# Score matmuls of a gated attention kernel: two on row halves at once, the third of a group over all 128 rows, the VectorE path's over all 128 rows, heads in alternating order

## The chip, the cores and the metric

The kernel runs on one core of one Trainium2 chip. The metric is device time in microseconds (us). Runs of one kernel on a chip are quoted as a median, and each is labelled fast when it lies within 1.5% of the fastest run of its kernel; only fast runs enter the ratios. A profile is of one execution; its span is about 2 us shorter than the measured time (1023.4 of 1025.38 us before).

## The reference

For x of 2048 x 512, the output is g * A(x) + (1 - g) * B(x) with g = sigmoid(x . gate_w).

- A is softmax attention with 32 heads of 16 channels: `scores = q k^T / 4`, `p = softmax(scores)`, `o = p v`, then a 512 x 512 output projection. The 32 x 2048 x 2048 exponentials are the bulk of all work.
- B is linear attention over softmax features of q and k, 32 features per head, with its own projections.

Everything is bf16 at the interface.

## The kernel before

Attention works on tiles of four heads and 512 queries (n counts the tiles, 32 in all). For each block of 128 keys, one score matmul per head writes a 128 x 512 result, which I call a unit. ScalarE exponentiates most units; of each tile's sixteen key blocks, one or two go to VectorE, which computes an approximate exponential. I call that the VectorE path: 224 of the 2048 units.

The ring of score results is a PSUM tile of 128 x 5 x 512 f32. I call each of its five parts of 128 x 512 a bank, so a unit fills one. Units go through it in groups of three and two banks in turn, and ScalarE takes one group per instruction:

```python
RING = 5
GROUPS = (3, 2)
...
deps = [self.o_exp[k - 2] if k >= 2 else None]      # a group's matmuls wait for the exp two groups back
...
def qk(x):
    n, kt, i = units[x]
    g = n % NG
    j = 64 * (i // 2)                               # heads 0, 1: rows 0-63; heads 2, 3: rows 64-127
    return lambda e: e.matmul(
        self.ps_ring[:, x % RING, :], self.kT[j:j + 64, g // 2, kt * P:(kt + 1) * P],
        self.qT[j:j + 64, n % 4, i % 2, :], start=True, stop=True, tile_position=(j, 0))
...
self.o_exp.append(s.op("act", ..., lambda e: e.activation(       # one exp over 3 or 2 banks
    self.ET[:, s0:s0 + w, :], self.ps_ring[:, b0:b0 + w, :], ACT.Exp, scale=float(DH) ** -0.5),
    deps, prio=tu))
```

kT holds the keys of eight heads, sixteen rows each. q of one head is stored with zeros in the other rows, so that a matmul over 64 rows of kT gives one head's scores. In the trace of before, two such matmuls on different row halves start 3 to 7 ns apart, so I take them to run at the same time; two on the same half start 219 to 227 ns apart. With heads in the order 0, 1, 2, 3, the halves run 0, 0, 1, 1, so half of the two-bank groups meet one half twice.

The value matmuls (17 columns: 16 channels and the row sum) take four heads side by side in four column quarters of the array; in the trace of before most of these start 3 or 4 ns after one another. A scheduler in Python puts all instructions into a fixed order per engine before the program is built; it uses assumed durations.

The softmax here doesn't subtract the row's maximum and nothing guards it: scores larger than these inputs give would overflow.

## Time and profile before

| | before |
|---|---|
| time | 1027.74 us, median of 3 (1026.12 to 1034.1) |
| span of the profile | 1023.4 us |
| mean granted TensorE clock | 0.832 |
| ScalarE at its own pace | 846 us |
| start and tail | 24 us |
| lost by ScalarE at full clock | 66 us of 683 |
| lost by ScalarE at half clock | 87 us of 317 |

The last four rows are worked out from the starts of ScalarE's instructions in the trace. I took the time from each start to the next. The first tenth of these times is ScalarE's own pace: 1.33 us after a three-bank exp, 0.90 us after a two-bank one, 0.48 us after a feature exp. Whatever is longer is lost, and it is booked under the clock that was granted at the later of the two starts, when the wait ends.

The page of the profile, cut to the header and the slices (one digit per fortieth of the span; PEclk is the granted clock in tenths):

```profile
span 1023.4 us, 12592 instructions
...
PE 882.4 (86%) x5216; PEld 220.3 (22%) x5216; DVE 774.7 (76%) x1082; ACT 881.6 (86%) x797; POOL 6.6 (1%) x12
...
ACT  4678578889888998899988989989899889999895
...
PEclk9878878898777888789988979957589698878775
```

Read ACT and PEclk together: ScalarE's thin slices stand where the clock is low. The costliest groups, with shapes kept apart (busy us, mean ns of one, then the idle time before them and what ended it):

```profile
L565 ACT ACTIVATE ET<-ps_ring 128x1536 bf16<-128x1536 f32 x365 | 539.6, 1478 | 100.3 <-PE ps_ring L551 95.1 <-PE ps_ot L585 2.5 <-PE ps_mp L615 0.8
L551 PE MATMUL ps_ring<-qT,kT 64*128 64x512 bf16 x1824 | 484.1, 445 | 100.7 <-ACT ET L565 95.3 <-DVE kT L492 2.3
L565 ACT ACTIVATE ET<-ps_ring 128x1024 bf16<-128x1024 f32 x364 | 383.5, 1053 | 17.6 <-PE ps_ring L551 12.5 <-PE ps_ot L585 3.9
```

Most of ScalarE's idle time stands before three-bank exps (100.3 us, against 17.6 before two-bank ones). (The means overlap a little: a three-bank exp lasts 1478 ns in the mean, and at ScalarE's own pace the next exp starts 1.33 us after its start.) Now five stretches from the table of stretches (PE, weight load, VectorE, ScalarE, GpSimd busy, then the granted clock):

```profile
130.00:300.00 170.00, 151.97 (x866) 37.24 (x865) 136.54 (x176) 145.43 (x136) 0.00 (x0) 0.83 0.01 3
300.00:500.00 200.00, 172.91 (x1033) 43.32 (x1031) 162.82 (x218) 180.74 (x168) 0.00 (x0) 0.86 0.01 4
500.00:700.00 200.00, 177.01 (x1099) 45.84 (x1096) 166.46 (x245) 182.91 (x167) 0.00 (x0) 0.87 0.02 7
700.00:900.00 200.00, 174.82 (x1059) 43.88 (x1055) 165.17 (x239) 182.61 (x166) 0.00 (x0) 0.83 0.02 6
...
950.00:975.00 25.00, 24.00 (x125) 4.97 (x121) 8.37 (x14) 21.77 (x20) 0.00 (x0) 0.73 0.00 1
```

The last row is the odd one: TensorE counts as busy for 24.0 of 25 us, and yet its clock is at half for part of the time. (The ends of matmuls are modelled in the profile, and a matmul at half clock counts as busy for longer: the median of a 64-row one is 606 ns, against 386 at full clock.) Long idle gaps aren't what stands there: from 130 us to 25 us before the end, no gap between TensorE's matmuls is longer than 1.3 us, and yet 82 windows of half clock lie in that stretch. The record of the granted clock knows in this trace only 1.0 and 0.5, in multiples of 3.413 us (but for the last entry, where the record ends); I call a stretch of 3.413 us on this grid a window.

What half clock does to a three-bank group, from the timeline (start, length, instructions, and in brackets the idle time before and what ended it; first at full clock, then at half; the last line is three exps in a row, with the form of the first):

```profile
501.96 0.60 PE L551 MATMUL ps_ring<-qT,kT 64*128 64x512 bf16 x3 [0.63 <-ACT ET L565]
```
```profile
956.64 1.04 PE L551 MATMUL ps_ring<-qT,kT 64*128 64x512 bf16 x3 [0.47 <-ACT ET L565]
...
957.71 4.03 ACT L565 ACTIVATE ET<-ps_ring 128x1536 bf16<-128x1536 f32 x3 [0.21 <-PE ps_ring L551]
```

Three matmuls take 0.60 us at full clock and 1.04 at half, and then ScalarE waits for them. The loop is: three-bank exp, its banks free, the next three-bank scores, the next three-bank exp. At full clock its fastest passage is 1.50 + 0.64 = 2.14 us. One pair of exps takes ScalarE 1.33 + 0.90 = 2.235 us, so TensorE has about 0.1 us to spare. I call this its slack.

### The profile page before, as it was taken

What the parts mean: (1) busy time and instruction counts of PE and PEld (TensorE: products, weight loads), DVE (VectorE), ACT (ScalarE), POOL (GpSimd) and SP (SyncE); (2) the same over time, 40 slices, a digit from 0 to 9 for tenths busy, and PEclk for the clock granted to TensorE, in tenths of its full rate; (3) what the DMA queues carried; (4) which work ended last, traced back from release to release, by engine and by line L of the source; (5) the groups of instructions that cost most, each with busy time, mean ns of one, the idle gap of its engine ahead of it and who ended that gap; (6) DMA issues with size and microseconds to landing.
All of it is one profiled execution on the core that took longest, in us unless ns stands there. A gap on an engine that the chain in (4) does not pass through costs nothing.

```text
span 1023.4 us, 12592 instructions
## 1 busy us (share of the span) xinstructions
PE 882.4 (86%) x5216; PEld 220.3 (22%) x5216; DVE 774.7 (76%) x1082; ACT 881.6 (86%) x797; POOL 6.6 (1%) x12
## 2 busy tenths in 40 slices
PE   6699888898889888988888898899988898888986
PEld 2122221222121221222222222212222222211111
DVE  3676787789777897789878979878788789877271
ACT  4678578889888998899988989989899889999895
POOL 2000000000000000000000000000000000000000
PEclk9878878898777888789988979957589698878775
DMA  5500000000000000000000000000000000000000
GB/s 124 126 6 2 1 6 1 6 1 1 6 1 6 1 1 5 1 6 6 11 6 11 6 6 11 11 1 1 2 5 1 5 16 12 3 3 1 1 1 21
DMA packets 25240, 11.25 MB, mean 11 GB/s; under 512 B 18080, under 2 KB 25184, under 8 KB 25184
## 3 DMA queue, kind: packets, MB, share of 16 engines
q1 hardware_dynamic: 23600, 10.06, 3.8%
q8 instruction: 41, 0.67, 0.3%
q10 hardware_dynamic: 1584, 0.39, 0.2%
q14 instruction: 15, 0.12, 0.0%
HBM read 3.16 MB, written 2.10 MB: 5 GB/s over the span
## 4 chain that ended last, share of the span: by engine, by line
PE 46%; ACT 43%; DVE 6%; SPq 4%; issue 1%; DMA 1%; ACTq 0%
ACT ET L565 40%; PE ps_ring L551 21%; PE ps_ot L585 8%; PE ps_mp L455 7%; PE ps_mp L615 3%; ACT phi L766 3%; PE ps_mp L845 3%; SPq L396 2%; PE ps_ot L644 1%; SPq L416 1%; DVE EW L621 1%; DVE ED L636 1%; DVE Ef L626 1%; DVE Em L631 1%; DVE Et L632 1%
## 5 line engine op out<-in xcount | busy, mean ns | idle before, releaser
L565 ACT ACTIVATE ET<-ps_ring 128x1536 bf16<-128x1536 f32 x730 | 850.8, 1265 | 117.9 <-PE ps_ring L551 107.6
L551 PE MATMUL ps_ring<-qT,kT 64*128 64x512 bf16 x1824 | 484.1, 445 | 100.7 <-ACT ET L565 95.3
L621 DVE TENSOR_SCALAR EW<-ps_mp 128x512 int32<-128x512 f32 x224 | 148.4, 682 | 86.6 <-PE ps_mp L615 75.9
L585 PE MATMUL ps_ot<-ET,Vaug 128*17 128x512 bf16 x1824 | 205.3, 443 | 4.8 <-DVE Vaug L502 2.2
L551 PEld LDWEIGHTS ps_ring<-qT,kT 64*128 64x128 bf16 x1824 | 86.0, 97 | 334.7 <-ACT ET L565 253.2
L636 DVE SCALAR_TENSOR_TENSOR ED<-EW,Et 128x1024 uint16<-128x1024 int32 x112 | 134.2, 1202 | 0.5 <-PE ps_ot L644 0.4
L615 PE MATMUL ps_mp<-qT,kT 64*128 64x512 bf16 x224 | 91.8, 440 | 13.1 <-DMA qT<-qst 7.4
L585 PEld LDWEIGHTS ps_ot<-ET,Vaug 128*17 128x17 bf16 x1824 | 44.1, 88 | 221.9 <-issue 201.4
L626 DVE TENSOR_SCALAR Ef<-EW 128x2048 f16<-128x2048 uint16 x56 | 68.2, 1218 | 1.2
L631 DVE TENSOR_TENSOR Em<-Ef,Em 128x2048 f16<-128x2048 f16 x56 | 68.1, 1216 | 0.0
L632 DVE TENSOR_TENSOR Et<-Et,Em 128x2048 f16<-128x2048 f16 x56 | 67.9, 1213 | 0.2
L655 DVE STREAM_TRANSPOSE T_79<-ps_ot 128x512 f32<-128x512 f32 x32 | 22.8, 713 | 57.8 <-PE ps_ot L585 57.4
L455 PE MATMUL ps_mp<-xT,WA 128*128 128x512 bf16 x128 | 43.5, 441 | 8.2 <-DMA xT<-in_A_x_dram 7.4
L766 ACT ACTIVATE phi<-ps_mp 128x512 bf16<-128x512 f32 x64 | 34.8, 599 | 9.9 <-PE ps_mp L455 9.9
L455 PE MATMUL ps_mp<-Wp,xT 128*128 128x512 bf16 x128 | 42.3, 415 | 0.9 <-DVE ob L810 0.9
L770 DVE TENSOR_REDUCE fsum<-phi 128x64 f32<-128x1024 bf16 x32 | 38.8, 1212 | 3.9 <-ACT phi L766 3.8
L772 DVE TENSOR_TENSOR phi<-phi,frec 128x1024 bf16<-128x1024 bf16 x32 | 38.8, 1212 | 0.0
L628 DVE TENSOR_SCALAR Em<-Ef 128x2048 f16<-128x2048 f16 x56 | 38.1, 680 | 0.7
L629 DVE TENSOR_SCALAR Et<-Ef 128x2048 f16<-128x2048 f16 x56 | 38.2, 682 | 0.0
L615 PEld LDWEIGHTS ps_mp<-qT,kT 64*128 64x128 bf16 x224 | 20.1, 97 | 67.1 <-issue 30.9
L644 PE MATMUL ps_ot<-ED,Vaug 128*17 128x512 bf16 x224 | 27.4, 502 | 1.4 <-DVE ED L636 1.4
L455 PE MATMUL ps_mp<-WA,xT 128*128 128x128 bf16 (+1 forms) x128 | 22.8, 298 | 3.2 <-DVE qT L471 1.7
(63 smaller groups left out, 375.9 us busy)
## 6 DMA issues: line engine op xcount, KB each, us to landing
out_dram<-outt SPq DMA_DIRECT2D x16, 128.0 KB, 1.7
qT<-qst SPq DMA_DIRECT2D x124, 16.0 KB, 1.8
WA<-in_A_wqkv_dram SPq DMA_DIRECT2D x3, 384.0 KB, 4.8
WBV<-in_B_wqkv_dram SPq DMA_DIRECT2D x1, 512.0 KB, 4.6
WoA<-in_A_wo_dram SPq DMA_DIRECT2D x1, 512.0 KB, 5.3
WoB<-in_B_wo_dram SPq DMA_DIRECT2D x1, 512.0 KB, 6.1
WA<-in_A_wqkv_dram ACTq DMA_DIRECT2D x3, 128.0 KB, 3.4
xT<-in_A_x_dram SPq DMA_TRANSPOSE x16, 2.7
```

The costliest lines, as they stand in the source:

```text
L455: m = s.op("pe", self.c_mm(n), lambda e, c=c: e.matmul(self.bk(b)[:, 0:n], lhs(c), rhs(c), start=(c == 0), stop=(c == 3)), deps if c == 0 ...
L551: return lambda e: e.matmul(self.ps_ring[:, x % RING, :], self.kT[j:j + 64, g // 2, kt * P:(kt + 1) * P], self.qT[j:j + 64, n % 4, i % 2, ...
L565: self.o_exp.append(s.op("act", w * 0.427 + 0.09, lambda e, b0=b0, s0=s0, w=w: e.activation(self.ET[:, s0:s0 + w, :], self.ps_ring[:, b0:b ...
L585: return lambda e: e.matmul(self.ps_ot[32 * i:32 * i + VSL, :], self.Vaug[:, kt, h, :], self.ET[:, (4 * p + i) % NSLOT, :], start=(kt == 0 ...
L615: m = s.op("pe", self.c_mm(512), lambda e, i=i, b=b: e.matmul(self.bk(b), self.kT[64 * (i // 2):64 * (i // 2) + 64, cp, kt * P:(kt + 1) * ...
L621: ws.append(s.op("dve", 0.76, lambda e, i=i, b=b: e.tensor_scalar(self.EW[:, ew.idx, i * QCH:(i + 1) * QCH], self.bk(b), float(EC), float( ...
L626: f = s.op("dve", 1.13, lambda e: e.tensor_scalar(self.Ef[:], lo(), float(2.0 ** -16), None, op0=ALU.mult), ws + [self.ed_prev], pr)
L631: u = s.op("dve", 1.13, lambda e: e.tensor_tensor(self.Em[:], self.Ef[:], self.Em[:], ALU.mult), [m1], pr)
L632: g_ = s.op("dve", 1.13, lambda e: e.tensor_tensor(self.Et[:], self.Et[:], self.Em[:], ALU.mult), [t, u], pr)
L636: vs.append(s.op("dve", 1.13, lambda e, c0=c0: e.scalar_tensor_tensor(out=self.ED[:, ed.idx, c0], in0=self.EW[:, ew.idx, c0], scalar=float ...
L766: ex.append(s.op("act", 0.53, lambda e, sg=sg: e.activation(self.phi[:, ph.idx, :, sg, :], self.bk(b).rearrange("p (h f) -> p h f", f=DH), ...
L770: rd = s.op("dve", 1.15, lambda e: e.tensor_reduce(self.fsum[:, fs.idx, :], flat(), AX.X, ALU.add), ex, r + 10)
```

## The change

The intent is to have TensorE do the score matmuls in pairs, and to have the third matmul of a group address all 128 rows. For that q is stored in a layout padded with zeros over all eight heads, with two buffers instead of four. The heads of a tile are taken in the order 0, 2, 1, 3, so that neighbours lie on different halves. The score matmuls of the VectorE path also go over all 128 rows. The core of the diff:

```diff
+ORDER = (0, 2, 1, 3)
...
-        at("qT", [P, 4, 2, QCH], bf)
+        at("qT", [P, 2, 4, QCH], bf)
...
-        units = [(n, kt, i) for n in range(NN) for kt in range(NT) if kt not in dve_tiles(n) for i in range(4)]
+        units = [(n, kt, i) for n in range(NN) for kt in range(NT) if kt not in dve_tiles(n) for i in ORDER]
...
-            def qk(x):
+            def qk(x, half):
                 n, kt, i = units[x]
                 g = n % NG
-                j = 64 * (i // 2)
+                r = slice(64 * (i // 2), 64 * (i // 2) + 64) if half else slice(0, P)
                 return lambda e: e.matmul(
-                    self.ps_ring[:, x % RING, :], self.kT[j:j + 64, g // 2, kt * P:(kt + 1) * P],
-                    self.qT[j:j + 64, n % 4, i % 2, :], start=True, stop=True, tile_position=(j, 0))
-            o_qk = s.op("pe", 0.36, [qk(x) for x in range(ua, ub + 1)], deps, prio=-1e5 + k, cols=256 * (ub - ua + 1))
+                    self.ps_ring[:, x % RING, :], self.kT[r, g // 2, kt * P:(kt + 1) * P],
+                    self.qT[r, n % 2, i, :], start=True, stop=True, tile_position=(r.start, 0))
+            w = ub - ua + 1
+            o_qk = s.op("pe", 0.25 if w == 2 else 0.47, [qk(x, w > 1 and x < ua + 2) for x in range(ua, ub + 1)],
+                        deps, prio=-1e5 + k, cols=512 if w == 2 else 1024)
...                                                        # the VectorE path
-                self.bk(b), self.kT[64 * (i // 2):64 * (i // 2) + 64, cp, kt * P:(kt + 1) * P],
-                self.qT[64 * (i // 2):64 * (i // 2) + 64, n % 4, i % 2, :], start=True, stop=True,
-                tile_position=(64 * (i // 2), 0)),
+                self.bk(b), self.kT[:, cp, kt * P:(kt + 1) * P], self.qT[:, n % 2, i, :], start=True, stop=True),
```

Cut: the placement of q in the new layout (by transfer, and for the first tile by four VectorE multiplies from SBUF, 0.35 us each, in place of two from PSUM at 0.74 us), and the matching order of the value matmuls. The new assumed durations (0.25 and 0.47 instead of 0.36) also reorder the instructions on every engine; `cols` is not read by the scheduler.

## The prediction

> **What bounds the kernel now.** ScalarE, whenever TensorE delivers in time. The groups of instructions show 729 exps, at best 1.33 us (three banks) or 0.90 us (two) from start to start; with 64 feature exps that is 846 us of work in a span of 1023. Start and tail take 24 us. The other 153 us are waits, mostly for the next score matmuls (table of waits: ScalarE behind ps_ring), and they follow TensorE's clock. The granted clock is 1.0 or 0.5, in multiples of 3.413 us; 0.5 holds for 34% of the span (mean 0.832). Half-clock stretches lose 87 us of 317, full-clock ones 66 of 683; some 30 us of that are start-up stalls (at 47 and 101 to 130 us), which stay. Long full-clock stretches (458 to 516 us) lose only some 2%.

> **What sets the clock.** I counted each window's matmul columns, weighted by the share of the array they address (64 rows 1/2; 17-column value matmuls 1/4). Of 196 full-clock windows one value, about 2,960[...], separates those followed by half clock from the others, with one exception. [...]this trace asks for array area.

> **What the change does.**
> - Activity: per five units the score matmuls count 4 x 256 + 512 = 1,536 instead of 1,280, and VectorE's 224 score matmuls 512 each instead of 256: 1.245 million columns instead of 1.094. Spread evenly over ScalarE's minimum time in program order, 13% of windows lie below 2,960 before, 4% after. Half-clock windows averaged 2,835, just too little to get out; 12% more lets most leave after one or two.
> - Two-bank groups always run on both halves (starts 3 ns apart); before, half of them serialised (219 ns). ScalarE hardly waits for these at full clock.
> - Cost: between 64-row and 128-row matmuls 306 to 316 ns pass from start to start instead of 216[...]. In three-bank groups the last starts 308 ns after the first instead of 226: +85 ns on the loop exp, scores, exp, which takes 2.14 us of a cycle of 2.235. Its slack is just eaten, so every TensorE delay ahead of such a group becomes a ScalarE wait; at half clock it costs some 150 ns. VectorE's score matmuls no longer run beside a ring pair: up to 45 us more TensorE time, mostly idle time.
> - Start: four small SBUF multiplies for two PSUM evictions, under 0.5 us.

> **Prediction.** Half clock falls to about 10%, mean clock 0.95. 846 work + 24 ends + 55 to 60 lost at full clock (20 to 30 of it start-up) + 28 lost at half clock = about 957 us; range 930 to 992. Faster by over 2%: 0.94; within 2%: 0.05; slower: 0.01.

> **What would show it.** Mean clock over 0.92; few half-clock windows after 130 us; ScalarE's wait for ps_ring down from 108 to 40-60 us; first to last start 308 ns in three-bank groups, 3 ns in two-bank ones; ScalarE's mean exp unchanged.

> **What would make it wrong.** If the throttle does not count the 128-row matmul's added rows, the clock stays at 0.83 and the time at 1020 to 1045. If the lost slack bites at every three-bank group, 975 to 995. If VectorE (775 us busy) cannot keep the faster pace, its value matmuls stall.

846 + 24 + 55 to 60 + 28 is 953 to 958, for which I put 957.

## The result

The changed kernel takes 973.02 us (median of 4, 972.26 to 974.33). Beside it, before had a median of 1030.49 us. The ratio is 0.9445, 95% interval 0.94 to 0.9491. Ratios here are the mean time of one kernel's fast runs over that of the other's of the same rounds, so not quite the ratio of the medians. The changed kernel is 5.6% faster, and the time lies in the predicted range, 16 us above its point of 957.

The same lines of the profile after, first the page:

```profile
span 972.5 us, 12590 instructions
...
PE 805.8 (83%) x5216; PEld 241.9 (25%) x5216; DVE 771.3 (79%) x1081; ACT 874.1 (90%) x797; POOL 6.6 (1%) x10
...
ACT  4688579899999999999999998999999999898895
...
PEclk9898799999999899999999998999999999878795
```

The costliest groups by shape:

```profile
L574 ACT ACTIVATE ET<-ps_ring 128x1536 bf16<-128x1536 f32 x365 | 531.4, 1456 | 64.8 <-PE ps_ring L558 60.8 <-PE ps_ot L595 0.8
L574 ACT ACTIVATE ET<-ps_ring 128x1024 bf16<-128x1024 f32 x364 | 373.6, 1026 | 16.0 <-PE ps_ring L558 12.3 <-PE ps_ot L595 3.5
L558 PE MATMUL ps_ring<-qT,kT 64*128 64x512 bf16 x1458 | 298.0, 405 | 118.6 <-ACT ET L574 112.8 <-DVE kT L494 2.1 <-DVE qT L470 0.4
...
L558 PE MATMUL ps_ring<-qT,kT 128*128 128x512 bf16 x366 | 149.8, 409 | 0.0
```

The stretches:

```profile
130.00:300.00 170.00, 146.66 (x942) 43.50 (x942) 150.42 (x193) 158.85 (x151) 0.00 (x0) 0.98 0.01 3
300.00:500.00 200.00, 167.23 (x1127) 50.51 (x1126) 174.91 (x238) 192.49 (x179) 0.00 (x0) 0.97 0.02 5
500.00:700.00 200.00, 168.85 (x1130) 51.40 (x1130) 168.96 (x253) 190.12 (x174) 0.00 (x0) 0.96 0.02 6
700.00:900.00 200.00, 168.01 (x1073) 49.03 (x1073) 162.98 (x231) 187.81 (x171) 0.00 (x0) 0.93 0.02 6
```

And a three-bank group, at full and at half clock (the view prints the form of the first matmul; the third has 128 rows):

```profile
503.80 0.71 PE L558 MATMUL ps_ring<-qT,kT 64*128 64x512 bf16 x3 [0.17 <-ACT ET L574]
```
```profile
874.66 1.15 PE L558 MATMUL ps_ring<-qT,kT 64*128 64x512 bf16 x3 [0.47 <-ACT ET L574]
```

The reader should see three things. The clock is up from 0.83-0.87 to 0.93-0.98 in every stretch, although TensorE's busy time fell from 882 to 806 us, 86 to 83% of the span; the mean clock over the span is 0.938. ScalarE's busy time per stretch rose with the clock (180.7 to 182.9 us of each 200 before, 187.8 to 192.5 after). And each three-bank group became slower, not faster: 0.71 us instead of 0.60 at full clock, 1.15 instead of 1.04 at half. The added time stands between the second matmul (64 rows) and the third (128 rows), 318 to 320 ns from start to start at full clock where two 64-row matmuls on the same half have 219 to 227; I call that step a mode switch.

| term of the span, us | before | predicted | after |
|---|---|---|---|
| ScalarE at its own pace | 846 | 846 | 853 |
| start and tail | 24 | 24 | 24 |
| lost at full clock | 66 | 55 to 60 | 55 |
| lost at half clock | 87 | 28 | 40.5 |
| sum | 1023 | 957 | 972.5 |

How the losses divide between the two clocks depends on the booking. Cut at 130 us, start-up loses 37 us before and 34 after. From there on half clock loses 69 us before and 19 after, full clock 48 and 44. Booked under the clock at the earlier start instead, the same stretch loses 88 and 21 at half clock, 29 and 41 at full. So the fall at half clock, 50 to 67 us, stands either way; whether full clock lost less or more doesn't.

### The profile page after: what moved, and what is told of

Read it like the earlier page. It is cut to its first block, busy times and chain, and to the rows that moved or that the text cites. A ratio compares the mean times of both kernels' runs of the same rounds, so it can differ in the third digit from the quotient of the medians.

```text
span 972.5 us, 12590 instructions
## 1 busy us (share of the span) xinstructions
PE 805.8 (83%) x5216; PEld 241.9 (25%) x5216; DVE 771.3 (79%) x1081; ACT 874.1 (90%) x797; POOL 6.6 (1%) x10
## 4 chain that ended last, share of the span: by engine, by line
ACT 47%; PE 35%; DVE 10%; SPq 5%; DMA 2%; issue 1%; ACTq 0%
ACT ET L574 44%; PE ps_ring L558 16%; PE ps_ot L595 6%; PE ps_mp L453 6%; PE ps_mp L625 3%; PE ps_mp L853 3%; ACT phi L774 3%; SPq L398 2%; DVE EW L629 2%; DMA qT<-qst 2%; SPq L483 1%; SPq L418 1%; DVE ED L644 1%; DVE Et L640 1%; DVE Em L639 1%
## 5 line engine op out<-in xcount | busy, mean ns | idle before, releaser
L558 PE MATMUL ps_ring<-qT,kT 64*128 64x512 bf16 (+1 forms) x1824 | 422.3, 406 | 118.6 <-ACT ET L574 112.8
L558 PEld LDWEIGHTS ps_ring<-qT,kT 64*128 64x128 bf16 (+1 forms) x1824 | 105.7, 94 | 423.9 <-ACT ET L574 259.5
L595 PE MATMUL ps_ot<-ET,Vaug 128*17 128x512 bf16 x1824 | 187.8, 404 | 2.5 <-ACT ET L574 1.3
L625 PE MATMUL ps_mp<-qT,kT 128*128 128x512 bf16 x224 | 85.2, 402 | 22.5 <-DMA qT<-qst 13.7
L453 PE MATMUL ps_mp<-xT,WA 128*128 128x512 bf16 x128 | 40.5, 415 | 8.5 <-DMA xT<-in_A_x_dram 7.4
L453 PE MATMUL ps_mp<-Wp,xT 128*128 128x512 bf16 x128 | 37.6, 382 | 0.6 <-DVE ob L818 0.3
L625 PEld LDWEIGHTS ps_mp<-qT,kT 128*128 128x128 bf16 x224 | 20.2, 97 | 65.7 <-issue 27.0
L652 PE MATMUL ps_ot<-ED,Vaug 128*17 128x512 bf16 x224 | 23.9, 420 | 2.7 <-DVE ED L644 2.5
```

What stands on the lines that cost most here:

```text
L453: m = s.op("pe", self.c_mm(n), lambda e, c=c: e.matmul(self.bk(b)[:, 0:n], lhs(c), rhs(c), start=(c == 0), stop=(c == 3)), deps if c == 0 ...
L558: return lambda e: e.matmul(self.ps_ring[:, x % RING, :], self.kT[r, g // 2, kt * P:(kt + 1) * P], self.qT[r, n % 2, i, :], start=True, st ...
L595: return lambda e: e.matmul(self.ps_ot[32 * i:32 * i + VSL, :], self.Vaug[:, kt, h, :], self.ET[:, (4 * p + k) % NSLOT, :], start=(kt == 0 ...
L625: m = s.op("pe", self.c_mm(512), lambda e, i=i, b=b: e.matmul(self.bk(b), self.kT[:, cp, kt * P:(kt + 1) * P], self.qT[:, n % 2, i, :], st ...
```

## The experiments

### Old matmuls in the new order

```diff
-ORDER = (0, 2, 1, 3)
+ORDER = (0, 1, 2, 3)
-... [qk(x, w > 1 and x < ua + 2) for x in range(ua, ub + 1)]
+... [qk(x, True) for x in range(ua, ub + 1)]
 # VectorE path: back to 64 rows
```

> The changed kernel's placement of q and its instruction order, but every score matmul on 64 rows again and the heads in their old order, so the addressed array area is that of before (1.094 million weighted columns). If the gain comes from the array area (my theory): mean granted clock 0.80 to 0.86, 1010 to 1045 us. If it comes from the new instruction order or the new q placement: about 973 us, clock near 0.94.

1030.82 us, ratio 1.0104 (1.0028 to 1.018), clock 0.816 in the profile. The new order and layout bring nothing; if anything they cost 1%. That rival falls.

### Pairs only

```diff
-... [qk(x, w > 1 and x < ua + 2) for x in range(ua, ub + 1)]
+... [qk(x, True) for x in range(ua, ub + 1)]
 # VectorE path: back to 64 rows; ORDER stays (0, 2, 1, 3)
```

> Heads alternate halves, all score matmuls on 64 rows: two-bank groups run as pairs, area as before. Area theory: clock 0.80 to 0.87, 1000 to 1035 us. Rival (the two matmuls at once and the shorter TensorE time are the gain): 960 to 985 us with the clock still low; three-bank groups last 226 ns from first to last start.

1012.6 us (997.16 to 1026.16), ratio 0.9821 (0.9694 to 0.9948), clock 0.861 in the profiled run and 0.811 to 0.838 in the others:

```profile
PEclk9798999899677887989789999899979996657775
```

Two of its four runs are slow and don't enter the ratio. Pairing alone gave 2.8% against the old matmuls by the two ratios, 18 us by the medians of all runs; the spread is wide, and most of the gain is missing. By the traces, its own gain lies at half clock: 69 us lost there against 113, while at full clock both lose 55 to 57. But the profile caught the fastest run of this kernel and the slowest of the other, so these two figures overstate it.

### Third matmul wide, VectorE path narrow

```diff
 # VectorE path: back to 64 rows; all else as the changed kernel
```

> As the changed kernel, but the VectorE path's score matmuls on 64 rows: 93 of the 151 thousand added columns stay. Area theory: clock between a2 and the changed kernel, 0.89 to 0.93, 978 to 1000 us. If only the ring's matmuls matter: 973 us as the changed kernel. If the shared rows of the VectorE path cost TensorE time that hurts: faster than 973 us.

980.85 us, ratio 0.9592 (0.9518 to 0.9667), clock 0.92. The third matmul's added rows are worth 2.3% over the pairs alone by the ratios (32 us by the medians), and the rows added in the VectorE path about 8 us more, by the changed kernel's 973; that second step compares chips and isn't shown by itself. Both steps go with the clock: 0.811 to 0.861, 0.917 to 0.931, 0.938 to 0.944 over each kernel's runs. The first of them is the cleanest test of the rows, for the number of matmuls and their columns stay the same.

### Swap: wide matmuls in the two-bank groups

```diff
-... [qk(x, w > 1 and x < ua + 2) for x in range(ua, ub + 1)]
+... [qk(x, w == 3) for x in range(ua, ub + 1)]
```

> The 128-row matmuls moved to the two-bank groups (both of them), three-bank groups all on 64 rows: area 1,792 per five units instead of 1,536, no mode switch inside a three-bank group (226 instead of 322 ns from first to last start), two-bank groups serial (216 ns instead of 3). Area theory with the eaten slack: clock 0.95 to 0.98, waits of ScalarE in full-clock stretches lower by 5 to 15 us, 945 to 962 us. Rival (pairing the two-bank groups is the gain): slower than 973 us, 985 or more.

960.66 us (956.99 to 962.49), ratio 0.9401 (0.9346 to 0.9456), clock 0.968. One part of my expectation missed: the time lost at full clock is 57.5 us, not less than the changed kernel's 55. What fell are the half-clock losses (33 instead of 40.5 us) and ScalarE's own pace (846 instead of 853 us). Run again beside the changed kernel on one chip:

> The swap kernel again beside the changed kernel on one chip: 955 to 964 us, clock about 0.97, so 1.0 to 1.6% faster than the changed kernel; if the earlier difference came from the chip, within 0.5% of it.

959.3 us, ratio 0.9365 (0.9324 to 0.9407).

> The changed kernel again, for a comparison on one chip: 968 to 978 us, clock about 0.94.

972.65 us, ratio 0.9494 (0.9444 to 0.9544). The six runs of each don't overlap (957.78 to 959.88 and 970.14 to 974.93); the medians are 1.4% apart. So the swap is the better form, and pairing the two-bank groups isn't needed for it. Its groups in the timeline: two-bank matmuls 128 rows wide, three-bank groups back at 0.60 us.

```profile
500.23 0.60 PE L558 MATMUL ps_ring<-qT,kT 128*128 128x512 bf16 x2
...
501.58 0.60 PE L558 MATMUL ps_ring<-qT,kT 64*128 64x512 bf16 x3
...
502.61 0.59 PE L558 MATMUL ps_ring<-qT,kT 128*128 128x512 bf16 x2
```

### Useless work: two-bank groups issued twice

```diff
-... [qk(x, w > 1 and x < ua + 2) for x in range(ua, ub + 1)]
+... [qk(x, True) for _ in range(2 if w == 2 else 1) for x in range(ua, ub + 1)]
```

> All score matmuls of the ring on 64 rows, and both matmuls of every two-bank group issued twice, the second time for nothing (the same result written again): the area of a4_swap, 1,792 per five units, by useless work. Area theory: clock 0.95 to 0.98 and within 1% of the swap kernel of this call, though 728 more matmuls than in a2_pairs_only (1013 us) run. Rival (less TensorE work or matmuls on all 128 rows are what helps): no faster than a2_pairs_only, clock 0.87 or less.

966.15 us, ratio 0.9438 (0.9391 to 0.9485), clock 0.979. It runs 728 more matmuls than the pairs-only kernel, whose results are thrown away, and is 46 us faster by the medians (ratios to before 0.9438 and 0.9821, on two chips):

```profile
span 966.0 us, 14046 instructions
...
PEclk9899799999999999999999999999999999999997
...
L558 PE MATMUL ps_ring<-qT,kT 64*128 64x512 bf16 x2552 | 444.4, 386 | 93.0 <-ACT ET L574 87.2 <-DVE kT L494 2.1 <-DVE qT L470 0.7
```

No ring matmul has 128 rows here, so it isn't that form that helps. More array area per window went with a higher clock (0.974 to 0.982 over the runs here, 0.811 to 0.861 with pairs only); TensorE's saved time is not the gain. Issuing twice also fills TensorE's time, so this run alone doesn't tell area from busy time; the count of windows below does. The kernel is 0.7% slower than the swap although its clock is a little higher: from 130 us on it loses 54 us at full clock where the swap loses 44. So extra TensorE work isn't free either.

### Everything wide: the mode switch back in the loop

```diff
-... [qk(x, w > 1 and x < ua + 2) for x in range(ua, ub + 1)]
+... [qk(x, w == 3 and x < ua + 2) for x in range(ua, ub + 1)]
```

> Both matmuls of a two-bank group and the third of a three-bank group on 128 rows: area 2,048 per five units, but the mode switch is back in the loop of the three-bank groups (322 instead of 226 ns). The clock should be no lower than in the swap kernel (0.965 or more). If the eaten slack of that loop costs time at full clock: 5 to 15 us slower than the swap kernel of this call. If it does not: equal within 3 us or faster.

965.22 us, ratio 0.9421 (0.9377 to 0.9465), clock 0.98: 5.9 us slower than the swap at no lower a clock. ScalarE's own pace is 853 us here as in the changed kernel, against 846 in the swap. At full clock at least 90% of the three-bank exps start 36 or 37 ns after the end of their last matmul, so they wait for it nearly every time; in the swap the median is 58 ns. This is the price of the eaten slack: about 7 us in the pace. From 130 us on the waits at full clock are 6 us longer too (50.5 against 44), and 5 us come back at half clock (3.5 against 8), so the 5.9 us are what is left of a larger price.

### Swap with the VectorE path narrow

```diff
 # as the swap; VectorE path: back to 64 rows
```

> The swap kernel with the VectorE path's score matmuls back on 64 rows: 57 thousand weighted columns less (1.281 instead of 1.338 million, still more than the changed kernel's 1.245), and these matmuls can run beside ring matmuls again. Area theory: clock 0.95 to 0.97, 957 to 966 us, so no gain over the swap kernel's 959 to 961. If the 128-row form of these matmuls costs TensorE time on the chain of waits: 950 us or less.

961.37 us, ratio 0.9371 (0.9337 to 0.9404), clock 0.96. No gain over the swap, whose ratios were 0.9401 and 0.9365 on the other two chips. The 45 us of TensorE time that I thought the wide form could cost doesn't show on the chain of waits.

### Swap with the old head order

```diff
-ORDER = (0, 2, 1, 3)
+ORDER = (0, 1, 2, 3)
 # wide matmuls as in the swap
```

> The swap kernel with the heads in the old order: the area of the swap kernel, but no group owes anything to alternating halves (two-bank groups are serial on 128 rows, three-bank groups need two turns in any order). If area alone is the gain: 955 to 966 us, clock 0.96 to 0.98. If alternating the halves is a cause of its own at full clock: 970 us or more.

959.79 us, ratio 0.9361 (0.9327 to 0.9395), clock 0.974. The same time as the swap's 959.3 to 960.66, across chips: the alternating order, half of the change's idea, isn't needed once the wide matmuls stand in the two-bank groups.

### The changed kernel without alternating heads

```diff
-ORDER = (0, 2, 1, 3)
+ORDER = (0, 1, 2, 3)
```

> The changed kernel with the heads in the old order: same area, but half of the three-bank groups now have both 64-row matmuls on the same half, so that their last matmul starts about 540 ns after the first instead of 322. Loop of these groups 2.47 us against ScalarE's 2.25: about 0.2 us on 182 groups, 1000 to 1012 us, with the clock still at 0.92 or more. If the clock falls to 0.87 or less instead, pairs and not area hold it up.

1044.21 us (1033.14 to 1052.61, two of six runs slow), ratio 1.0131 (1.0078 to 1.0184), clock 0.918 in the profile. The clock, 0.892 to 0.927 over the six runs, came out a little under the 0.92 that I expected and well over 0.87; the time missed by more than 30 us. In its profile (1033 us) ScalarE lost 106 us at full clock instead of 55, in some 185 waits over 60 ns before three-bank exps (86 in the changed kernel), where I had expected 182 late groups. I had put the added loss at about 40 us and it is 51 at full clock, with 8 more at half. A late group from the timeline, 0.92 us long:

```profile
706.82 0.92 PE L558 MATMUL ps_ring<-qT,kT 64*128 64x512 bf16 x3 [0.69 <-ACT ET L574]
```

So a high clock alone doesn't make the kernel fast: at 0.918 this kernel is no faster than before at 0.83 (1.3% slower by the ratio). In the changed kernel the alternation is needed, because it pays for the third matmul's mode switch: with it a three-bank group takes 0.71 us at full clock, and a late one without it 0.92. Why four of the other five runs of this kernel are another 11 to 19 us slower than the profiled one isn't settled beyond their lower clocks (0.892 to 0.908 in the four slower runs).

### Swap with the late loads

```diff
 # as the swap, and four weight loads on the same queue (branch B's projections, both output
 # projections) get a release of 36 us in the scheduler's own reckoning:
+    ... self.WBT[...] ..., 0.84, rel=36.0)   # 8 transposed loads
+    ... self.WBV, self.WoA, self.WoB ..., rel=36.0)
```

> The swap kernel with branch B's transposed weights and three 512 KB weight loads issued after the second head's q placement, not before it. If the stall near 47 us (8 to 11 us) is that transfer waiting behind those loads: the stall is gone, 949 to 955 us. If something else holds TensorE there: 957 to 962 us and the stall moves at most.

952.44 us (951.49 to 954.48), ratio 0.9293 (0.926 to 0.9325), the best kernel. This edit does move instructions. The queue in the swap, then here:

```profile
25.73 10.84 SPq L418 DMA_TRANSPOSE WBT<-in_B_wqkv_dram  x8
36.62 0.58 SPq L420 DMA_DIRECT2D WBV<-in_B_wqkv_dram  x1
37.25 0.51 SPq L421 DMA_DIRECT2D WoA<-in_A_wo_dram  x1
37.80 0.51 SPq L423 DMA_DIRECT2D WoB<-in_B_wo_dram  x1
38.42 17.32 SPq L483 DMA_DIRECT2D qT<-qst  x8
```
```profile
27.80 2.50 SPq L483 DMA_DIRECT2D qT<-qst  x4
30.34 10.63 SPq L418 DMA_TRANSPOSE WBT<-in_B_wqkv_dram  x8
```

The second tile's q went out at 27.8 instead of 38.4 us, and ScalarE ran through the stretch where it had stood for 7.6 us. Not all of that arrived: the later stall of the VectorE chain, near 113 us in the swap's first run, came near 101 us and was 10.7 us long instead of 8.3. The gain is 7 us against the swap with the old order on the same chip (959.79).

## Why the prediction was right, and where it was off

**ScalarE bounds the kernel and TensorE's clock sets its waits: right.** The changed kernel's span is 50.9 us shorter; by the table 46.6 us of that is ScalarE time no longer lost at half clock, 11.4 us no longer lost at full clock, and 7 us were added to ScalarE's pace. The half-clock part is at least that large under either booking; the full-clock part isn't sure even in its sign. The 55 us at full clock hit the number in part by luck: I had put 20 to 30 us of start-up into them, and they hold 12, with 44 from 130 us on.

**The clock follows the addressed array area: right, and now tested.** With rows and columns weighted as in the prediction and the line at 2,960, the trace of before has 1 wrong window in 196, that of the changed kernel 3 in 245, that of the useless-work kernel 1 in 268, and that of the all-wide kernel none in 268. The line came from one trace and sorts the windows of kernels made afterwards; with the two repeats (changed kernel and swap) it is wrong for 6 of 1,483 windows. TensorE's busy time is the rival: counting the part of a window in which any matmul streams (216 ns for 512 columns), the best line for all six traces is wrong 35 times, and the best one for before alone 10 times in 196. The same 2,960 also sorts the half-clock windows, those above it being followed by full clock: wrong for 11 of 221, if a matmul there is spread over twice the time. Below the line lie 33 windows before and 14 after, 17% and 6%, where I had predicted 13% and 4%. That a more fitting weighting exists isn't excluded; the weights were chosen by what separated the windows of before best. At 216 ns for each 512 columns a window of 3.413 us would hold some 8,090, so the line lies at about 37% (an estimate from those two numbers of the trace).

**"12% more lets most leave after one or two": right between start-up and tail, but with 5% more area, not 12.** Over all windows it looks wrong: the half-clock windows after have 2,752 weighted columns on average, less than the 2,835 of before, and 14 of 34 were followed by full clock (33 of 99 before). But 13 of these 34 lie before 130 us or in the last 25 us, where TensorE stands (the waits of 8.4 us at 47 us and 8.3 us at 113 us) or runs out of work, and a standing TensorE addresses nothing. Between them there are 21 half-clock windows where before had 82. They have 3,051 columns on average (2,916 before), 11 of the 21 were followed by full clock (29 of 82 before), and 8 of the 11 half-clock stretches lasted one or two windows (15 of 29 before). That a three-bank group takes 542 ns from first to last start at half clock, and took 405, fits the smaller rise: more area per group came with longer groups. No run tests that by itself.

**The half-clock loss: larger than forecast, but its size hangs on the booking.** Half clock holds for 12% of the windows, not 10, and loses 40.5 us, not 28; by the table this is the larger term of the 16 us, beside the 7 us of pace. But 22 of the 40.5 us lie before 130 us, mostly in stalls that are booked whole under one clock, and booked under the clock at the earlier start half clock loses 29 us and full clock 68. So which clock took the missing 9 us stays open.

**The third matmul's cost: right in kind, a little larger.** From first to last start a three-bank group has 322 ns where I said 308; the switch inside the ring is 318 to 320 ns. I said that the slack would just be eaten. It was overdrawn by some 20 ns per pair, which is the 7 us in ScalarE's pace that I had left at 846. The all-wide kernel against the swap shows it alone. My case "the lost slack bites at every three-bank group" thus came close to true, for at full clock three quarters of the changed kernel's three-bank exps start 36 or 37 ns after their last matmul; it cost 20 ns each time and not the 18 to 38 us that I had set for it. In the traces 318 to 320 ns stand at full clock where 216 to 227 are usual, and at half clock 535 to 539 where some 400 are; why the step is longer, no run shows.

**Pairs bring little to ScalarE at full clock: right.** Starts in two-bank groups are 3 to 4 ns apart at full clock. But pairing alone was worth some 18 us by the medians of widely spread runs, by the traces at half clock, which the prediction didn't mention, and inside three-bank groups it is what makes the change work at all.

**Signs.** ScalarE's wait for the ring fell from 108 to 73 us, not to 40-60; the mean clock is 0.938, over the 0.92 that I asked for. The half-clock windows between 130 us and the last 25 us are 21, and were 82. ScalarE's mean exp was to stay and fell a little, from 1478 to 1456 ns (three banks) and from 1053 to 1026 (two). The start-up stalls stayed, as said. VectorE kept the pace: it is busy 771 us in the shorter span.

## What to carry to other kernels

When a granted clock stands in the profile, look at it by stretches before reading any wait: here 87 of 153 lost us were booked at half clock, and matmuls over zero rows (1012.6 to 980.85 us for the third matmul's), even matmuls issued twice for nothing (1012.6 to 966.15 us), made the kernel faster. Put such work where there is slack (here the two-bank groups), not in the loop that sets the pace, where a mode switch cost 7 us of pace. A part of a change that is needed in one form (the head order) can be worthless in the next, so undo parts one at a time.
